# A DFT and two small MLPs on one core: the first weights' sums by DMA, their middle row by way of DRAM, another place for Qo's second operand and for the second MLP's PSUM tiles

## The chip, the cores and the metric

The kernel runs on one core of a Trainium2 chip. The metric is the time of one execution on the device, in microseconds. The engines are named as the profile names them: PE (TensorE, matrix products; PEld is its weight loading), DVE (VectorE), ACT (ScalarE), POOL (GpSimd), and SP, which mostly issues DMA transfers. POOL issues transfers too.

## The reference

The program takes `x` of 4 batches x 3072 positions x 256 channels and computes the real part of a two-dimensional DFT, then an MLP with a leaky activation, then a second MLP with a shift by one position and a gate.

```python
X = np.fft.fft(np.fft.fft(x, axis=1), axis=2).real
h = X @ w_in
X = np.maximum(0.01 * h, h) @ w_out
xk = mu_k * X + (1 - mu_k) * X_prev
xr = mu_r * X + (1 - mu_r) * X_prev
k = np.maximum(xk @ w_k, 0)
out = (k * k @ w_v) / (1 + np.exp(-(xr @ w_r)))
```

`X_prev` is X moved by one position, with zeros in front; the hidden widths are 2048 and 1024. The weights `w_in`, `w_out`, `w_k`, `w_v` and `w_r` arrive as float64, `x` as float32.

## The kernel before

**Products in two parts.** PE multiplies float32r operands. Where a product has to be exact to float32, each operand is split into a high and a low part (`hi_lo`: ACT copies the high part, DVE subtracts it, L90), and three products are added in PSUM: high by high, high by low, low by high.

**The DFT.** The transform along the 3072 positions is folded by symmetry into four real kinds, Pe, Qe, Po and Qo, each a set of matmuls with a table (`tab_a` to `tab_d`, 1158 KB each, loaded by POOL, L166). One kind is made in two halves, `fft_a` and `fft_b`, called at chosen units; `fft_src` splits the operands (t1Qo, sh1Qo, sl1Qo for batch 1), and DVE's L300 and L302 form the two classes of each kind (c1Po and the like). Pe has a middle row besides, which `fft_a` adds with one f32 matmul (L287, `e7p` by `altt`). The transform along the 256 channels isn't done by itself: it is multiplied into `w_in` at the start, by the tables `cet` and `sot` (matmuls L363 and L365 into `wps`), and the folded weights are kept as `woh`, `wol`, `weh`, `wel`.

**Units of the first MLP.** The four batches have four classes each (A1, A2, G1, G2), a class has 16 units of 128 hidden channels. `i` counts the 64 units of a batch. For each unit PE multiplies with Q (`mm_b`, 3 matmuls, L539), begins the next unit with P (`mm_a`, 3 matmuls, L527), and does the output product of an earlier unit (`outmm`, 12 matmuls, L550). Between these stand DVE's d (L591), ev (L532, for the next unit: a row of c times a column of `w128` is added, so it needs both) and gl (L571), and ACT's two leaky activations (L86) and gh (L83). PE's `mm_b` of a unit waits for that unit's ev.

**The boot.** There is no time in which the weights alone are loaded: the float64 weights are loaded in eight pieces each, converted and split while batch 0 is transformed and while the first class runs. `boot(u)` puts one step behind each of the first 16 units. A float64 piece goes through the steps `one` (ACT L108, DVE L110), `two` (DVE L116, makes fv), `three` (DVE L119, ACT L122, POOL L123, makes the small rest r), `four` (ACT L136 makes the high part, POOL L137 adds fv to r) and `five` (DVE L141 makes the low part). The column of `w128` for a piece of `w_in` is taken by `w_in_row`: PE multiplies the parts `wh` and `wl` with a column that is 1 in its first place only (L383, L384, four matmuls of two columns for a piece), and ACT copies the result.

**The second weights.** `w_k`, `w_v` and `w_r` make nine pieces, with the same five steps at one a unit: five pieces at units 53 to 57 of batches 0, 1 and 2 and at units 0 to 4 of batches 1 and 2, four in batch 3 from unit 8 on.

**The c rows.** Channel 128 of the folded channels has a row of its own: its transform along the positions is a row c, made by `c_a` and `c_b` (L405 to L417), stored to DRAM (L418) and spread over 128 partitions by `load_c`; its folded weights are the columns `w128`. ev adds the product of both.

**The second MLP** starts behind the last unit. `k_mm` (L854), `r_mm` (L904) and `v_mm` (L896) are its products. Its PSUM tiles are taken from a pool `ps2`, which is opened when the pools `ps_s` and `ps_o` of the first have been released, so its first `kps` waits for the last copies out of them (`flush`, yo). `do_prep(ti)` lists the steps that make the next tile's operands (mt, mx, mh, ml), and one step is taken a slot; a slot is the work around one `k_mm`, 12 matmuls.

All loops are unrolled. The order on each engine is that of the program; what an engine waits for is worked out from the tiles. The units at which the DFT's kinds stand, and the slots of the second MLP (f1 is that of `do_prep`), are these numbers:

```python
po_u, qo_u, f0, f1 = (2, 10, 17, 50) if b == 0 else (1, 4, 14, 50)
pe_u, qe_u = 53, 56
...
f0, f1, g0 = (0, 2, 4) if ti else (2, 5, 5)
```

Of the kernel before, what the change touches and what calls it, by code (L numbers as in the profile page):

```python
# [56 lines left out]
def fft_mlp_kernel(ctx, tc, xa, xb, x7, x8, x87, tb, tbs, alt, ce, so, mu, w_in, w_out, w_k, w_v, w_r, out):  # L57
# [5 lines left out]
    yd = [[[dram.tile([P, 2, JP], F32, name=f"y{b}_{c}_{s}") for s in range(2)] for c in range(4)] for b in range(B)]  # L63
    cd = dram.tile([B, 4, JP], F32, name="cd")

    ps_s = tc.alloc_tile_pool(name="ps_s", bufs=4, space=PSUM)
# [4 lines left out]
    w128 = misc.tile([P, NF], F32, name="w128")  # L71
    one0 = misc.tile([P, 2], F32R, name="one0")
    misc.tile([P, 112], F32, name="pad0")
    wp = tc.alloc_tile_pool(name="wp", bufs=1)
# [58 lines left out]
    def split_steps(z, k, f, parts):  # L133
        def four():
            z["p"] = parts()
            A.activation(z["p"][0], z["f"], ACTF.Copy, scale=2.0 ** -8)  # L136
            G.tensor_tensor(z["r"], z["r"], z["f"], op=ALU.add)  # L137

        def five():
            hi, lo = z["p"]  # L140
            V.scalar_tensor_tensor(lo, z["r"], 2.0 ** -8, hi.bitcast(F32), op0=ALU.mult, op1=ALU.subtract)  # L141
        return (*f64_steps(z, k, f), four, five)
# [114 lines left out]
    def fft_src(b, kind, h):  # L257
# [25 lines left out]
    def fft_a(b, kind):  # L283
        ps = ps_s.tile([P, 512], F32, tag="s", name=f"f{b}{kind}")
        fft_mm(b, kind, 0, ps, kind != "Pe")
        if kind == "Pe":
            T.matmul(ps[:, :JP], e7p, altt, start=False, stop=True)  # L287
        ev = work.tile([P, JP], F32, tag="fv", bufs=2, name=f"fe{b}{kind}")
        act_copy(ev[:, :JP], ps[:, :JP])
        return ps, ev  # L290
# [42 lines left out]
    uoh, uol = ([wp.tile([P, HF, D], F32R, name=n)] for n in ("uoh", "uol"))  # L333
    V.memset(one0.bitcast(F32), 0.0)
    V.memset(one0[0:1].bitcast(F32), 1.0)
    V.memset(altt, 0.0)
# [39 lines left out]
    def w_in_row(q):  # L376
        if q >= 8:
            return
        ps = win.pop(q)[0]
        for i in range(2):  # L380
            f = slice((2 * q + i) * P, (2 * q + i + 1) * P)
            o = ps[:, 2 * i:2 + 2 * i]
            T.matmul(o, woh[:, f], one0, start=True, stop=False)  # L383
            T.matmul(o, wol[:, f], one0, start=False, stop=True)  # L384
        act_copy(w128[:, 2 * q:2 * q + 2], ps[:, 0:4].rearrange("p (i t) -> p i t", t=2)[:, :, 0])

# [96 lines left out]
    ca = c_a(c8p, "a", True)  # L483
    w_in_row(1)
    w_in_parts(2)
    fft_b(0, "Pe", *pe)
    wout[0][1]()
    cs0 = c_b(c8p, "b", A1, *ca)
    cur_c = load_c(0, A1)
    wout[1][0]()  # L490
    qe = fft_a(0, "Qe")
    wout[0][2]()
    next_pair()
    w_in_parts(3)
    wout[1][1]()
    fft_b(0, "Qe", *qe)
    next_pair()
    cur = split_class(0, A1, "P") + split_class(0, A1, "Q")
    w_in_mm(2)


    def boot(u):
        q = u // 2
        if u % 2 == 0:
            w_in_row(q + 2)
            w_in_mm(q + 3)
            if 0 < q < 7:
                wout[q + 1][2]()
            if q < 6:
                wout[q + 2][0]()  # L510
            w_in_load(q + 4)
        else:
            w_in_split(q + 3)
            if q < 6:
                wout[q + 2][1]()
            w_in_parts(q + 4)
            w_out_load(q + 3)


# [238 lines left out]
    w_in_split(2)  # L758
    wout[1][2]()
    for b in range(B):  # L760

        po_u, qo_u, f0, f1 = (2, 10, 17, 50) if b == 0 else (1, 4, 14, 50)
        pe_u, qe_u = 53, 56
        done = 0
# [113 lines left out]
    wp.release()  # L878
    ps_o.release()
    ps_s.release()  # L880


    ps2 = ctx.enter_context(tc.tile_pool(name="ps2", bufs=1, space=PSUM))
    p2 = w2["p2"] = ctx.enter_context(tc.tile_pool(name="p2", bufs=2))
# [13 lines left out]
    def r_mm(xr, sig, m):  # L898
        hi, lo = xr
        ps = ps2.tile([P, 512], F32, tag="rps", bufs=2, name="rps")  # L900
        i = 0
# [21 lines left out]
    def drain():  # L923
        if q2:
            t, f, kk = q2.pop(0)
            if f == 0:
                t["v"] = [ps2.tile([P, 512], F32, tag="v", bufs=4, name=f"v{m}") for m in range(NB)]
            v_mm(f, kk, t["v"])
# [7 lines left out]
    for ti in range(len(tiles)):  # L936
        rd = ready.pop(ti)
        t = {"i": ti, "sig": p2.tile([P, NB, J], F32, tag="sig", name="sig")}
        end = ti == len(tiles) - 1
        f0, f1, g0 = (0, 2, 4) if ti else (2, 5, 5)  # L940
        if ti == 0:
            q1.append((t, 1, early[1][2]))
            q2.append((t, 0, kk0))
        for f in range(f0, NK):
            ps = ps2.tile([P, 512], F32, tag="k", bufs=2, name="kps")
            r = p2.tile([P, J], F32, tag="r", bufs=3, name="rl")
# [106 lines left out]
```

## Time and profile before

| | us |
|---|---|
| three runs | 1532.92, 1531.22, 1531.23 |
| median | 1531.23 |
| the profiled execution | 1529.78 |
| its span in the trace | 1528.0 |
| PE busy | 1499.0 (98%) |
| DVE busy | 1078.4 (71%) |
| ACT busy | 927.7 (61%) |
| POOL busy | 172.0 (11%) |

The span runs from the first to the last instruction of the trace; 1.78 us of the execution lie outside it. Busy times are sums over an engine's instructions, and a matmul is counted until its modelled end, so that two neighbours overlap: PE's idle time is best read from the list of its waits. A row of the timeline gives start, duration, engine, line, operation and operands, and in brackets the idle time of the engine ahead of it with what ended that. Names in rows leave buffer numbers out.

### The profile page before, as it was taken

Reading aid. Unit: us, or ns where it says so; the run is one execution under the profiler, and the core shown is the slowest. Engines: PE = TensorE matmul, PEld = TensorE weight load, DVE = VectorE, ACT = ScalarE, POOL = GpSimd, SP = SyncE. Lnnn points to the kernel's source line nnn. Section 1 sums busy time; section 2 is a strip of 40 time slices with the busy share of each in tenths; the row PEclk is TensorE's granted clock in tenths of the full one; section 3 lists DMA queues with packets and bytes.
Section 4 is the critical chain, followed back from the end, with each engine's and each line's share of the span. In section 5 each row is a group of like instructions: output and inputs, shape, how many; then the busy total and the mean of one; then the engine's idle time right before and its main releaser. Section 6 shows DMA issues by size and latency. Waiting matters only on the chain.

```text
span 1528.0 us, 22618 instructions
## 1 busy us (share of the span) xinstructions
PE 1499.0 (98%) x8490; PEld 1473.8 (96%) x8490; DVE 1078.4 (71%) x1798; ACT 927.7 (61%) x1785; POOL 172.0 (11%) x165
## 2 busy tenths in 40 slices
PE   5899999999999999999999999999999999999999
PEld 2789999999999999999999999999999999999998
DVE  7876767766667766667777666777677777776775
ACT  2666656656666665656566656666666666666664
POOL 4444201132101132001001000000000000000000
PEclk8999999999999999999999999999999999999999
DMA  7427405464214653124411002111111111111100
GB/s 249 156 83 149 82 10 164 129 153 90 55 27 152 183 119 56 40 75 138 137 54 47 21 1 73 42 42 42 42 42 42 42 42 42 42 42 42 42 22 32
DMA packets 74295, 116.34 MB, mean 76 GB/s; under 512 B 10798, under 2 KB 53822, under 8 KB 71114
## 3 DMA queue, kind: packets, MB, share of 16 engines
q1 hardware_dynamic: 51082, 74.62, 15.6%
q0 software_dynamic: 23104, 40.29, 11.8%
q8 instruction: 66, 1.08, 0.3%
q14 instruction: 43, 0.35, 0.1%
HBM read 87.06 MB, written 27.83 MB: 75 GB/s over the span
## 4 chain that ended last, share of the span: by engine, by line
PE 96%; DVE 2%; ACT 1%; issue 1%; DMA 0%; SPq 0%; POOL 0%; ACTq 0%; DVEq 0%
PE o L550 35%; PE kps L854 17%; PE v L896 17%; PE ps L539 9%; PE ps L527 9%; PE rps L904 4%; PE wps L363 0%; PE cps L405 0%; DMA xl<-in_xb 0%; PE cps L414 0%; PE f0Qo L280 0%; PE f0Po L280 0%; PE f1Qo L280 0%; PE f2Qo L280 0%; DVE fo L214 0%
## 5 line engine op out<-in xcount | busy, mean ns | idle before, releaser
L591 DVE SCALAR_TENSOR_TENSOR d<-ev,ps 128x384 f32<-128x384 f32 (+1 forms) x256 | 141.6, 553 | 195.8 <-PE ps L539 195.8
L83 ACT ACTIVATE gh<-g 128x768 fp32r<-128x768 f32 (+1 forms) x256 | 216.3, 845 | 69.7 <-PE o L550 67.7
L858 ACT ACTIVATE rl<-kps 128x384 f32<-128x384 f32 x254 | 124.9, 492 | 218.7 <-PE kps L854 218.7
L571 DVE TENSOR_TENSOR gl<-g,gh 128x768 fp32r<-128x768 f32 (+1 forms) x256 | 251.3, 982 | 1.3 <-ACT gh L83 1.0
L86 ACT ACTIVATE g<-ps 128x384 f32<-128x384 f32 (+1 forms) x256 | 125.9, 492 | 192.2 <-DVE d L591 191.2
L859 DVE SCALAR_TENSOR_TENSOR k<-kps,rl 128x384 f32<-128x384 f32 x254 | 141.5, 557 | 137.6 <-ACT rl L858 133.8
L550 PE MATMUL o<-gh,uoh 128*128 128x384 f32 (+1 forms) x1024 | 228.0, 337 | 0.0
L550 PE MATMUL o<-gl,uoh 128*128 128x384 f32 (+1 forms) x1024 | 227.7, 337 | 0.0
L550 PE MATMUL o<-gh,uol 128*128 128x384 f32 (+1 forms) x1024 | 227.6, 337 | 0.0
L550 PEld LDWEIGHTS o<-gl,uoh 128*128 128x128 f32 x1024 | 182.9, 188 | 0.0
L550 PEld LDWEIGHTS o<-gh,uoh 128*128 128x128 f32 x1024 | 182.6, 188 | 0.0
L550 PEld LDWEIGHTS o<-gh,uol 128*128 128x128 f32 x1024 | 182.5, 188 | 0.0
L532 DVE SCALAR_TENSOR_TENSOR ev<-cb,w,ps 128x384 f32<-128x384 f32 (+1 forms) x256 | 157.1, 614 | 0.0
L90 DVE TENSOR_TENSOR k2l<-k,k2h 128x384 fp32r<-128x384 f32 x254 | 139.6, 550 | 0.4 <-ACT k2h L83 0.4
L896 PE MATMUL v<-k2h,wvl 128*128 128x384 f32 x510 | 134.5, 334 | 0.0
L896 PE MATMUL v<-k2h,wvh 128*128 128x384 f32 x510 | 134.5, 334 | 0.0
L896 PE MATMUL v<-k2l,wvh 128*128 128x384 f32 x510 | 134.5, 334 | 0.0
L86 ACT ACTIVATE g<-d 128x384 f32<-128x384 f32 (+1 forms) x256 | 132.6, 518 | 0.0
L83 ACT ACTIVATE k2h<-k 128x384 fp32r<-128x384 f32 x254 | 131.7, 518 | 0.0
L854 PE MATMUL kps<-mh,wkh 128*128 128x384 f32 x508 | 129.1, 335 | 1.3 <-ACT mh L83 0.7
L854 PE MATMUL kps<-ml,wkh 128*128 128x384 f32 x508 | 129.0, 334 | 0.0
L854 PE MATMUL kps<-mh,wkl 128*128 128x384 f32 x508 | 128.9, 334 | 0.0
(377 smaller groups left out, 2551.0 us busy)
## 6 DMA issues: line engine op xcount, KB each, us to landing
out_dram<-o SPq DMA_DIRECT2D x31, 384.0 KB
y<-yo SPq DMA_DIRECT2D x24, 384.0 KB
tab_a<-in_tbs POOLq DMA_DIRECT2D x6, 1158.0 KB, 5.4
tab_b<-in_tbs POOLq DMA_DIRECT2D x6, 1158.0 KB, 5.9
tab_c<-in_tbs POOLq DMA_DIRECT2D x6, 1158.0 KB, 8.2
tab_d<-in_tbs POOLq DMA_DIRECT2D x6, 1158.0 KB, 5.7
xl<-in_xa SPq DMA_DIRECT2D x24, 256.0 KB
xa<-y SPq DMA_DIRECT2D x16, 384.0 KB
```

The lines of the kernel that those rows point to most:

```text
L83: A.activation(o, i, ACTF.Copy)
L86: A.activation(o, i, ACTF.Prelu, alpha=0.01)
L90: V.tensor_tensor(lo, src, hi.bitcast(F32), op=ALU.subtract)
L527: T.matmul(x["ps"][:, :n], l[:, f], r[:, :n], start=(i == 0), stop=(i == 2))
L532: V.scalar_tensor_tensor(x["ev"][:, :n], x["cb"][:, :n], w128[:, u:u + 1], x["ps"][:, :n], op0=ALU.mult, op1=ALU.add)
L539: T.matmul(x["ps"][:, :n], l[:, f], r[:, :n], start=False, stop=(i == 2), skip_group_check=True)
L550: T.matmul(po[s][h][:, :n], w[:, u % HF, h * P:(h + 1) * P], g[:, s, :n], start=(u == 0 and i == 0), stop=(u == NF - 1 and i == 2))
L571: V.tensor_tensor(gl[:, :, :n], x["g"][:, :, :n], x["gh"][:, :, :n].bitcast(F32), op=ALU.subtract)
L591: V.scalar_tensor_tensor(d[:, :n], x["ev"][:, :n], 2.0, x["ps"][:, :n], op0=ALU.mult, op1=ALU.subtract)
L854: T.matmul(ps[:, :J], w[:, k, sl], x[:, k], start=(i == 0), stop=(i == 5))
L859: V.scalar_tensor_tensor(k2, ps[:, :J], 0.0, r, op0=ALU.max, op1=ALU.mult)
L896: T.matmul(vps[m][:, :J], w[:, f, m * P:(m + 1) * P], x, start=(f == 0 and i == 0), stop=(f == NK - 1 and i == 2))
```

## The change

- `four` adds fv to r by a DMA that POOL issues (`accum_op=add`, 256 KB, from SBUF to SBUF) instead of a POOL instruction. This holds for the eight pieces of `w_out` and the nine of the second weights. In the boot, `five` moves from the even units to the odd ones, behind `w_in_split`.
- `w_in_row` has no matmuls: ACT copies row 0 of the PSUM tile, SP stores it to DRAM (`wd`), and `w_in_col`, a unit later, loads it back as a column.
- Fourteen matmuls on a tile of zeros ("warm") stand ahead of the first weights.
- The first c row is spread by a matmul with a row of ones (`spread_c`) and a copy by ACT, without DRAM.
- P of the first class is split behind `fft_b` of Pe instead of together with Q.
- Pe's middle row is multiplied in float32r for batches 1 to 3: two matmuls, for which ACT and DVE split `e7p`'s first row.
- Qo's unit goes from 4 to 5 (batches 1 to 3), Qe's from 56 to 57.
- The second MLP takes its PSUM tiles from the first's pools, and for tile 0 `do_prep(1)` comes at slot 4, not 5.

```diff
...
             A.activation(z["p"][0], z["f"], ACTF.Copy, scale=2.0 ** -8)
-            G.tensor_tensor(z["r"], z["r"], z["f"], op=ALU.add)
+            G.dma_start(z["r"], z["f"], accum_op=ALU.add)
...
         srcs[b, kind, h] = hi, lo
+        if kind == "Pe" and h == 0:
+            m = work.tile([1, 2, P], F32R, tag="fv", bufs=2, name=f"e7r{b}")
+            hi_lo(m[:, 0], m[:, 1], e7p[0:1])
+            a = work.tile([1, JP], F32R, tag="fv", bufs=2, name=f"altr{b}")
+            act_copy(a, altt[0:1])
+            srcs[b, "mid"] = m, a
...
         fft_mm(b, kind, 0, ps, kind != "Pe")
-        if kind == "Pe":
+        if kind == "Pe" and b == 0:
             T.matmul(ps[:, :JP], e7p, altt, start=False, stop=True)
+        elif kind == "Pe":
+            m, a = srcs.pop((b, "mid"))
+            for i in range(2):
+                T.matmul(ps[:, :JP], m[:, i], a, start=False, stop=(i == 1))
...
+
+    def spread_c(cs):
+        ps = ps_s.tile([P, 512], F32, tag="s", name="cbp")
+        T.matmul(ps[:, :JP], ones, cs[0:1, 0], start=True, stop=True)
+        t = pqp.tile([P, JP], F32, tag="cb", bufs=2, name="cb0_0")
+        act_copy(t[:, :JP], ps[:, :JP])
+        return t
+
...
             return
-        ps = win.pop(q)[0]
-        for i in range(2):
-            f = slice((2 * q + i) * P, (2 * q + i + 1) * P)
-            o = ps[:, 2 * i:2 + 2 * i]
-            T.matmul(o, woh[:, f], one0, start=True, stop=False)
-            T.matmul(o, wol[:, f], one0, start=False, stop=True)
-        act_copy(w128[:, 2 * q:2 * q + 2], ps[:, 0:4].rearrange("p (i t) -> p i t", t=2)[:, :, 0])
+        row = fft.tile([1, 256], F32, tag="x7", bufs=1, name="wr")
+        act_copy(row, win.pop(q)[0][0:1, 256:512])
+        Q.dma_start(wd[q:q + 1], row)
+
+    def w_in_col(q):
+        if q < 8:
+            Q.dma_start(w128[:, 2 * q:2 * q + 2], wd[q].rearrange("(i p) -> p i", p=P))
...
     vt, gt = (("g", 2), ("g", 2), ("yo", 2)), (("gh", 2), ("gl", 2), ("sd", 2))
+    zero = uoh[0][:, 0:2]
+    V.memset(zero.bitcast(F32), 0.0)
+    ones = work.tile([1, P], F32, tag="sd", bufs=2, name="ones")
+    G.memset(ones, 1.0)
...
     w_out_load(2)
+
+    ps = ps_s.tile([P, 512], F32, tag="s", name="warm")
+    for i in range(14):
+        T.matmul(ps, zero[:, 0, 0:P], zero, start=True, stop=True)
...
     pe = fft_a(0, "Pe")
     ca = c_a(c8p, "a", True)
     w_in_row(1)
+    w_in_col(0)
     w_in_parts(2)
     fft_b(0, "Pe", *pe)
+    cur = split_class(0, A1, "P")
     wout[0][1]()
+    w_in_col(1)
     cs0 = c_b(c8p, "b", A1, *ca)
-    cur_c = load_c(0, A1)
+    cur_c = spread_c(cs0)
     wout[1][0]()
     qe = fft_a(0, "Qe")
-    wout[0][2]()
     next_pair()
     w_in_parts(3)
     wout[1][1]()
+    wout[0][2]()
     fft_b(0, "Qe", *qe)
     next_pair()
-    cur = split_class(0, A1, "P") + split_class(0, A1, "Q")
+    cur += split_class(0, A1, "Q")
     w_in_mm(2)
     def boot(u):
         q = u // 2
         if u % 2 == 0:
+            w_in_load(q + 4)
             w_in_row(q + 2)
             w_in_mm(q + 3)
-            if 0 < q < 7:
-                wout[q + 1][2]()
             if q < 6:
                 wout[q + 2][0]()
-            w_in_load(q + 4)
         else:
             w_in_split(q + 3)
+            if q < 7:
+                wout[q + 1][2]()
             if q < 6:
                 wout[q + 2][1]()
             w_in_parts(q + 4)
             w_out_load(q + 3)
+            w_in_col(q + 2)
...
     w_in_split(2)
-    wout[1][2]()
...
-        po_u, qo_u, f0, f1 = (2, 10, 17, 50) if b == 0 else (1, 4, 14, 50)
-        pe_u, qe_u = 53, 56
+        po_u, qo_u, f0, f1 = (2, 10, 17, 50) if b == 0 else (1, 5, 14, 50)
+        pe_u, qe_u = 53, 57
...
     wp.release()
-    ps_o.release()
-    ps_s.release()
-
-
-    ps2 = ctx.enter_context(tc.tile_pool(name="ps2", bufs=1, space=PSUM))
+
+
...
             if f == 0:
-                t["v"] = [ps2.tile([P, 512], F32, tag="v", bufs=4, name=f"v{m}") for m in range(NB)]
+                t["v"] = [ps_o.tile([P, 512], F32, tag=f"o{t['i'] % 2}{m}", name=f"v{m}") for m in range(NB)]
...
         end = ti == len(tiles) - 1
-        f0, f1, g0 = (0, 2, 4) if ti else (2, 5, 5)
+        f0, f1, g0 = (0, 2, 4) if ti else (2, 4, 5)
...
         for f in range(f0, NK):
-            ps = ps2.tile([P, 512], F32, tag="k", bufs=2, name="kps")
+            ps = ps_s.tile([P, 512], F32, tag="s", name="kps")
...
```

The order of instructions moves at three places that matter. On DVE in the boot, from the classes of Pe to the first ev, this stood before (`c0Pe` and `c0Qe` are the classes, `cs` is the first c row, `Pl` and `Ql` the low parts of the first class, `uol` is what `five` writes):

```order
L417 SCALAR_TENSOR_TENSOR cs<-cev,cps 4x386
L110 TENSOR_SCALAR h<-h 128x512
L116 SCALAR_TENSOR_TENSOR fv<-st,h 128x512
L119 TENSOR_SCALAR h<-fv 128x512
L141 SCALAR_TENSOR_TENSOR uol<-r,uoh 128x512
L110 TENSOR_SCALAR h<-h 128x512
L116 SCALAR_TENSOR_TENSOR fv<-st,h 128x512
L119 TENSOR_SCALAR h<-fv 128x512
L302 SCALAR_TENSOR_TENSOR c0Qe_401<-fe0Qe,c0Qe_400 128x386
L90 TENSOR_TENSOR Pl_0_410<-c0Pe_352,Ph_0_409 128x386
L90 TENSOR_TENSOR Ql_0_414<-c0Qe_400,Qh_0_413 128x386
L532 SCALAR_TENSOR_TENSOR ev<-cb_0_365,w_105,ps 128x386
```

Here `five` (L141) stood between the two float64 pieces, and Pl next to Ql. On DVE at the same place there stands now:

```order
L90 TENSOR_TENSOR Pl_0_370<-c0Pe_365,Ph_0_369 128x386
L433 SCALAR_TENSOR_TENSOR cs<-cev,cps 4x386
L110 TENSOR_SCALAR h<-h 128x512
L116 SCALAR_TENSOR_TENSOR fv<-st,h 128x512
L119 TENSOR_SCALAR h<-fv 128x512
L110 TENSOR_SCALAR h<-h 128x512
L116 SCALAR_TENSOR_TENSOR fv<-st,h 128x512
L119 TENSOR_SCALAR h<-fv 128x512
L141 SCALAR_TENSOR_TENSOR uol<-r,uoh 128x512
L312 SCALAR_TENSOR_TENSOR c0Qe_421<-fe0Qe,c0Qe_420 128x386
L90 TENSOR_TENSOR Ql_0_430<-c0Qe_420,Qh_0_429 128x386
L560 SCALAR_TENSOR_TENSOR ev<-cb_0_385,w_106,ps 128x386
```

Pl has moved up ahead of cs, and `five` behind the steps of the next float64 piece. On POOL in batch 1's first units there stood (`tab_c` and `tab_d` are tables, `r` the rest of a float64 piece):

```order
L166 DMA tab_c_2922<-in_tbs 128x2316
L123 TENSOR_TENSOR r<-st,h 128x512
L166 DMA tab_d_3013<-in_tbs 128x2316
L137 TENSOR_TENSOR r<-r,fv 128x512
L166 DMA tab_a<-in_tbs 128x2316
```

The addition was POOL's own. On POOL at the same place there stands now:

```order
L166 DMA tab_c_2938<-in_tbs 128x2316
L123 TENSOR_TENSOR r<-st,h 128x512
L166 DMA tab_d_3029<-in_tbs 128x2316
L137 DMA r<-fv 128x512
L166 DMA tab_a<-in_tbs 128x2316
```

The addition has become a transfer, in the same queue as the tables. On DVE at this place there stood (`wl` is what `five` writes; `d`, `ev` and `gl` are a unit's):

```order
L300 SCALAR_TENSOR_TENSOR c1Po_3010<-fe1Po,c1Po_3009 128x386
L264 TENSOR_TENSOR t1Qo_3015<-pm_1042 128x384
L266 TENSOR_TENSOR t1Qo_3015<-x_1_1049 1x128
L90 TENSOR_TENSOR sl1Qo_3017<-t1Qo_3015,sh1Qo_3016 128x384
L591 SCALAR_TENSOR_TENSOR d<-ev,ps 128x386
L532 SCALAR_TENSOR_TENSOR ev<-cb_0_2360,w_105,ps 128x386
L571 TENSOR_TENSOR gl<-g,gh 128x2x386
L141 SCALAR_TENSOR_TENSOR wl<-r,wh 128x512
```

The operand t1Qo came right behind the class c1Po. On DVE at this place there stands now:

```order
L310 SCALAR_TENSOR_TENSOR c1Po_3026<-fe1Po,c1Po_3025 128x386
L619 SCALAR_TENSOR_TENSOR d<-ev,ps 128x386
L560 SCALAR_TENSOR_TENSOR ev<-cb_0_2370,w_106,ps 128x386
L599 TENSOR_TENSOR gl<-g,gh 128x2x386
L264 TENSOR_TENSOR t1Qo_3067<-pm_1052 128x384
L266 TENSOR_TENSOR t1Qo_3067<-x_1_1059 1x128
L90 TENSOR_TENSOR sl1Qo_3069<-t1Qo_3067,sh1Qo_3068 128x384
L141 SCALAR_TENSOR_TENSOR wl<-r,wh 128x512
L619 SCALAR_TENSOR_TENSOR d<-ev,ps 128x386
L560 SCALAR_TENSOR_TENSOR ev<-cb_0_2370,w_106,ps 128x386
```

The operand t1Qo has moved behind the d, ev and gl of a unit, with `five` behind it as before.

## Rows read from the trace of the kernel before

**Rows 1.** The page: busy time, share of the span and instructions of each engine.

```profile
PE 1499.0 (98%) x8490; PEld 1473.8 (96%) x8490; DVE 1078.4 (71%) x1798; ACT 927.7 (61%) x1785; POOL 172.0 (11%) x165
```

**Rows 2.** PE's waits in the whole run: line waited for, total us, times, longest.

```profile
PE wps L363 <- DVE fv L116: 14.7, 2, 8.2
...
PE f1Qo L280 <- ACT sh1Qo L83: 0.9, 1, 0.9
...
PE f2Qo L280 <- ACT sh2Qo L83: 0.9, 1, 0.9
```

**Rows 3.** Windows: span, then busy (count) of PE, PEld, DVE, ACT, POOL; clock; DMA.

```profile
62.00:110.00 48.00, 48.00 (x249) 41.17 (x248) 38.49 (x63) 30.67 (x60) 19.91 (x15) 1.00 0.30 95
```

**Rows 4.** Timeline of PE in the boot: start, duration, operation, count, [idle before <-releaser].

```profile
49.48 0.42 PE L539 MATMUL ps<-Qh,wh 128*128 128x386 f32 x1 [1.54 <-DVE ev L532]
...
50.62 0.17 PE L383 MATMUL wps<-one,wh 128*128 128x2 f32 x1
...
50.98 1.11 PE L363 MATMUL wps<-fv,cet 128*128 128x256 f32 x4
```

**Rows 5.** Timeline of the boot: ACT, POOL and DVE, same columns.

```profile
39.08 0.48 ACT L83 ACTIVATE cs<-cps 4x386 f32<-4x386 f32 x1 [1.03 <-PE cps L414]
...
46.80 1.59 POOL L137 TENSOR_TENSOR r<-r,fv 128x512 f32<-128x512 f32 x1
...
47.18 1.63 DVE L90 TENSOR_TENSOR Ql<-c0Qe,Qh 128x386 fp32r<-128x386 f32 x1
```

**Rows 6.** Timeline of all engines, batch 1's first units.

```profile
296.78 0.34 PE L539 MATMUL ps<-Qh,wh 128*128 128x386 f32 x1
...
297.25 0.58 POOL L166 DMA_DIRECT2D tab_d<-in_tbs  x1 [2.25 <-PE f1Po L280]
...
297.51 2.08 DVE L300 SCALAR_TENSOR_TENSOR c1Po<-fe1Po,c1Po 128x386 f32<-128x386 f32 x1 [1.69 <-ACT c1Po L83]
...
297.85 1.31 POOL L137 TENSOR_TENSOR r<-r,fv 128x512 f32<-128x512 f32 x1
...
302.98 0.34 PE L539 MATMUL ps<-Qh,wh 128*128 128x386 f32 x1
...
303.35 0.68 DVE L141 SCALAR_TENSOR_TENSOR wl<-r,wh 128x512 fp32r<-128x512 f32 x1
...
306.16 0.33 PE L539 MATMUL ps<-Qh,wh 128*128 128x386 f32 x1
```

**Rows 7.** Landing of Pool's transfers: a page row, then min/median/max of line L202.

```profile
tab_d<-in_tbs POOLq DMA_DIRECT2D x6, 1158.0 KB, 5.7
...
L202 POOL DMA_DIRECT2D xl<-in_xb x18: 1073/1091/1859, 119.5 to 611.3; - x18
...
DMA to landing us min/median/max: 4.3/4.9/9.5
```

**Rows 8.** Line L166 from 320.9 to 321.5 with its landing; timeline of POOL behind it.

```profile
L166 POOL DMA_DIRECT2D tab_b<-in_tbs x1: 947/947/947, 321.0 to 321.0; - x1
...
DMA to landing us min/median/max: 8.9/8.9/8.9
...
322.39 1.80 POOL L202 DMA_DIRECT2D xl<-in_xb  x1
```

**Rows 9.** Timeline of POOL and DVE, a weight piece in batch 3.

```profile
760.92 1.49 POOL L137 TENSOR_TENSOR r<-r,fv 128x512 f32<-128x512 f32 x1
...
766.57 0.56 DVE L591 SCALAR_TENSOR_TENSOR d<-ev,ps 128x386 f32<-128x386 f32 x1 [0.56 <-PE ps L539]
```

**Rows 10.** Timeline of PE around Pe's middle row, batch 0's last units.

```profile
244.32 0.81 PE L287 MATMUL f1Pe<-altt,e7p 128*128 128x386 f32 x2
...
245.14 0.34 PE L539 MATMUL ps<-Ql,wh 128*128 128x384 f32 x1
```

**Rows 11.** Timeline of PE at the second MLP's start.

```profile
925.36 0.62 PE L854 MATMUL kps<-mh,wkh 128*128 128x384 f32 x2 [0.58 <-ACT yo L83]
...
941.25 0.61 PE L854 MATMUL kps<-mh,wkh 128*128 128x384 f32 x2 [0.74 <-ACT mh L83]
```

More of the change, by code (lines that the diff above doesn't have):

```diff
@@ L64, in fft_mlp_kernel @@
     cd = dram.tile([B, 4, JP], F32, name="cd")
+    wd = dram.tile([8, 256], F32, name="wd")
     ps_s = tc.alloc_tile_pool(name="ps_s", bufs=4, space=PSUM)
@@ L71, in fft_mlp_kernel @@
     w128 = misc.tile([P, NF], F32, name="w128")
-    one0 = misc.tile([P, 2], F32R, name="one0")
-    misc.tile([P, 112], F32, name="pad0")
+    misc.tile([P, 120], F32, name="pad0")
     wp = tc.alloc_tile_pool(name="wp", bufs=1)
@@ L333, in fft_mlp_kernel @@
     uoh, uol = ([wp.tile([P, HF, D], F32R, name=n)] for n in ("uoh", "uol"))
-    V.memset(one0.bitcast(F32), 0.0)
-    V.memset(one0[0:1].bitcast(F32), 1.0)
     V.memset(altt, 0.0)
@@ L899, in r_mm @@
         hi, lo = xr
-        ps = ps2.tile([P, 512], F32, tag="rps", bufs=2, name="rps")
+        ps = ps_s.tile([P, 512], F32, tag="s", name="rps")
         i = 0
@@ L976, in fft_mlp_kernel @@
         w2[k].release()
+    ps_o.release()
+    ps_s.release()
 def dft_tables():
```

## The prediction

> **What bounds the kernel now.** I read the page first. TensorE (PE) is busy 98% of the span, 1499.0 us [rows 1], VectorE (DVE) 71% and ScalarE (ACT) 61%; so a change is worth what it takes from PE's own work or from PE's idle time, and work of other engines counts only where PE comes to wait for it. The list of PE's waits says where the idle time lies: 14.7 us of it in two waits for the first folded-weight matmuls, before any table has come, and 0.9 us in each of batches 1 and 2 on the second operand of Qo [rows 2]. The windows then separate the stages: between 62 and 110 us PE has no gap at all (48.00 of 48.00), with 0.30 of the DMA in use [rows 3]. There an instruction taken from PE shortens the run by its own length, and a wait put in lengthens it. Before 62 us PE and the three vector engines pass work to and fro [rows 4, 5], and a gain must survive every hand-over. The last views are the timelines of two places with gaps, batch 1's first units [rows 6] and the second MLP's start [rows 11].
>
> All sums are made against the profiled run, 1529.78 us; the median of the three runs is 1531.23, and I carry the difference over unchanged. A difference under 0.2%, 3.1 us, is one that a measurement of this kernel can't tell from none.
>
> **The change part by part.**
>
> *Boot, up to 62 us.* The f32 matmul that spreads the first c row stands between the matmuls of cps and those of f0Qe, and it waits for ACT's cs. Before, f0Qe followed cps at once, at about the time at which cs started, 39.0; cs ends at 39.56 [rows 5]. One group of four row matmuls falls out ahead of it, 50.98 − 50.62 = 0.36 [rows 4], so cs ends at about 39.2 now. The spreading matmul has no row of its own; its nearest is Pe's middle row, also f32 with 386 columns: 0.65 us (below, [rows 10]). f0Qe then starts at 39.85: +0.9 at this point, and Qh and Ql behind it are later by as much, less the 0.5 that Ph no longer takes on ACT ahead of Qh. Ql started at 47.18 and took 1.63 us while POOL's sum ran beside it [rows 5]; d, with as many elements, takes 0.56 [rows 9]. With the sum off POOL, Ql runs from 47.6 to 48.1, ev to 48.7, and unit 0's mm_b, which had to wait 1.54 us for that ev [rows 4], starts then instead of at 49.48: 0.8 ahead. Two more row groups (0.36 each) are gone before 62: 1.5 ahead at best. DVE and POOL don't get ahead by as much, so PE's later waits on them grow; I keep **−0.9**, and from −1.9 (every small wait gone) to +0.6 (the spreading matmul's 0.9 stays and only one row group is felt).
>
> *Four row groups behind 62 us.* Four of the eight stand where PE is full [rows 3, 4]: 4 × 0.36 = **−1.4**. The row now goes ACT, DRAM, column; ACT and SP have the time (ACT's share is in [rows 1]), and a column is asked for two units before its use.
>
> *Pe's middle row in float32r.* From 244.32 to the second matmul behind it is 0.82, of which one matmul of 0.18 is that behind it: 0.65 for the f32 row. A unit's 18 float32r matmuls take 306.16 − 302.98 = 3.18 [rows 6], 0.177 each; two are 0.35. Three batches × 0.29 = **−0.9**. The three small ACT copies and one DVE operation for it lie in a unit that has room: nothing.
>
> *Qo a unit later.* A unit's start at 296.78 comes back at 302.98, 6.20 later. One unit (3.18) and the nine matmuls of f1Qo (9 × 0.177 = 1.59) explain 4.77: 1.43 are lost, first to c1Po on DVE, 2.08 us long because POOL's sum began at 297.85 beside it, then to the operand behind c1Po [rows 6]. With a unit more of room, and no sum on POOL, this goes; batch 2 has the same wait [rows 2]. 2 × 1.43 = **−2.9**.
>
> *The sums by DMA.* POOL's seventeen additions become transfers that add 256 KB in SBUF. Most are asked for a unit or more before DVE's subtraction (`five`) needs them, in the boot over ten us before for most pieces: nothing. Two are close, in batch 1 and 2 at unit 3. POOL issues tab_d at 297.25, the sum behind it at 297.85 [rows 6]; `five` now waits for a transfer, and behind it on DVE stand d and ev of the next unit, for which PE waits. PE reaches that ev's use at 296.78 + 2 × 3.18 + 1.59 = 304.73. DVE needs about 1.7 from `five` to the end of that ev (0.68 for `five` [rows 6], 0.56 for d [rows 9] and as much again for ev, a little overlapped). So the sum must have landed by 303.0, 5.2 us after its issue. The trace shows no sum inside SBUF. Its nearest row is Pool's sum from DRAM of the same 256 KB, L202: 4.3 to 9.5 us to landing, median 4.9 [rows 7]. But here a table of 1158 KB, 5.7 us to landing [rows 7], stands ahead of it, landing at 302.95. One such pair is in the trace: tab_b at 321.00, 8.9 to landing, and a sum issued behind it at 322.39 [rows 8], which is the 9.5 of L202; it landed 2.0 after the table, behind another of 128 KB. 256 KB alone at tab_d's rate are 5.7 × 256/1158 = 1.3 us, so our sum lands at 304.2: 1.2 late, twice: **+2.4**. The ends: nothing (4.9 after issue is in time), and 2 × (9.5 − 5.2) = +8.6.
>
> L202's issue on POOL took 1.07 us in the middle and 1.86 at most [rows 7], 0.8 more. The Trainium skill, DMA: Bandwidth & Descriptors, section SWDGE vs HWDGE vs iDMA, says that GpSimd writes such descriptors into SBUF and that VectorE's two-port mode shuts it out of there; that speaks against the change. No row ties the 1.86 to it; by that rule I would add at most 0.8 to each of the two sums, 1.6 in all, which stands inside the ends above.
>
> *Second MLP's start.* Without the release of the pools, kps doesn't wait for the copy yo, idle 0.58; and the second operand, mh, comes a slot sooner (12 matmuls, 2.1 us), which is more than PE's wait for it, 0.74 idle [rows 11]. A matmul is listed with 0.34 where the next starts 0.177 behind it [rows 6], so each such gap really takes 0.16 more: 0.58 + 0.74 + 0.32 = 1.6. The pairs at these waits take 0.62 and 0.61 instead of 0.34 + 0.177 = 0.52, and mh's second half comes behind its first; for that I add 0.4. Together **−2.0**, from −1.0 (mh is held up elsewhere) to −2.2.
>
> *At nothing:* the fourteen dummy matmuls, which fill part of the 14.7 us in which PE waits for weights [rows 2]; if that cover is gone they cost what reaches past the first weights, under 2 us. Qe a unit later: its successors are not waited for.
>
> Sum: −0.9 − 1.4 − 0.9 − 2.9 + 2.4 − 2.0 = **−5.7**: a profiled run of 1524.1, a median of **1525.5**.
>
> **The rivals.**
>
> *A: the two sums land in time.* For it: L202's median of 4.9 is under 5.2 [rows 7], and a transfer within SBUF has no DRAM to wait for. Against it: the table ahead in the same queue. The 2.4 goes: −8.1, **1523.1**. The Trainium skill, same page, section Queues, rings and completion order, says that each DMA engine takes descriptors in ring order; by that rule A falls, and the one pair in the trace agrees, its sum 2.0 us behind its table [rows 8].
>
> *B: the two sums are as late as L202's slowest.* 9.5 us instead of 6.4: −5.7 − 2.4 + 8.6 = +0.5, **1531.7**, no difference. For it: the 9.5 was seen behind a table [rows 8]; against it: that table itself took 8.9, tab_d here 5.7.
>
> *C, slower: sums within SBUF are slow in themselves.* Then not two, but all nine w2 pieces hold up DVE. In batch 3 the sum was issued at 760.92, d started at 766.57 [rows 9]; PE's next use is about 2.6 later, less DVE's 1.7: the sum is needed by 767.5, 6.6 after issue. With seven such pieces and the two at 5.2, a landing of x us costs 2(x − 5.2) + 7(x − 6.6) against the gain of 8.1: even at x = 7.2, slower by over 0.2% from 7.5 on, and at 9.5 it is 8.6 + 20.3 − 8.1 = +20.8, **1552**. Against it: no row here is that slow in the middle.
>
> *D: the boot change does nothing or loses, all else as forecast.* The spreading matmul's 0.9 is not given back: 1.5 us later, 1527.0; that lies inside the forecast.
>
> **How the numbers follow.** The forecast (with D) 0.52, A 0.22, B 0.16, C 0.10. The forecast's own range, with the boot from −1.9 to +0.6 and the second MLP from −1.0 to −2.2, is 1524.3 to 1528.0. The range of 8 in 10 goes down through A with a good boot, 1521.9, and up to half of B's way, 1530.0; it leaves out C and the later half of B. Faster by over 0.2% (below 1528.2): the forecast and nearly all of A, 0.73; within 0.2%: most of B, 0.16; slower: C and a little of B, 0.11.
>
> **What would show it.** In the changed profile: PE's waits on sh1Qo, sh2Qo, yo and mh are gone, and no small matmuls with 2 columns are left. c1Po takes 0.56. In batch 1 and 2 a wait of PE for ev of about 1.2 stands near 304 and at the like place of batch 2, with DVE's `five` ended late by a DMA: that decides between the forecast, A and B. If DVE waits for DMA at `five` in batch 3 as well, C is right. The boot is right if f0Po starts near 61.2. I would be wrong if TensorE's granted clock fell in a stretch where it was full before, since PE's rows would then lengthen all over that stretch.

## The result, and where it went

The changed kernel takes 1541.82 us, the median of four runs (1541.13 to 1543.13), against 1531.22: a ratio of 1.0071, with an interval of 1.0059 to 1.0083, 10.6 us slower. I had forecast 1525.5 and a range that ended at 1530.0. The profiled execution has a span of 1539.7 us, 11.7 more than before.

PE's busy time grows by 5.9 us, and the chain shows the new thing: besides PE, which falls from 96% to 92%, DMA stands in it with 3%. From the page after, as [rows 1] before, and the chain's line:

```profile
PE 1504.9 (98%) x8474; PEld 1479.2 (96%) x8474; DVE 1073.8 (70%) x1800; ACT 930.8 (60%) x1792; POOL 160.4 (10%) x166
...
PE 92%; DVE 3%; DMA 3%; issue 1%; POOL 1%; ACT 0%; SPq 0%; POOLq 0%; ACTq 0%; DVEq 0%
```

The list of PE's waits after answers [rows 2] (line waited for, total us, times, longest):

```profile
PE ps L567 <- DVE ev L560: 13.7, 7, 3.5
PE wps L379 <- DVE fv L116: 10.1, 2, 8.7
PE f0Pe L293 <- DVE e7p L238: 3.0, 1, 3.0
```

The waits for sh1Qo, sh2Qo, yo and mh are gone, as forecast. In their place PE waits 13.7 us in seven places for ev, up to 3.5 us at a time. Before, the waits for ev were 2.3 us in two places.

Where PE stands at the start of each unit's second operand (its first L539 or L567 matmul), after less before, splits the difference by place:

| from | to | us |
|---|---|---|
| start | unit 0 | −1.8 |
| unit 0 | unit 3 | +1.7 |
| unit 3 | unit 11, the row groups | −1.3 |
| units 53 to 60 of batches 0 to 2 (the middle row) | | +0.2 |
| units 62 and 63 of batches 0 to 2 | | +5.2 |
| units 4 to 8 of batches 1 and 2: Qo's wait gone | | −2.9 |
| the same units: sums | | +12.5 |
| the rest of the first MLP | | 0.0 |
| the second MLP | | −2.0 |

The total is +11.7 (the entries are rounded). Two entries carry it. The first is batch 1's unit 6; the timeline after, as [rows 6] before:

```profile
297.62 0.57 POOL L166 DMA_DIRECT2D tab_d<-in_tbs  x1 [2.26 <-PE f1Po L286]
...
297.88 0.56 DVE L310 SCALAR_TENSOR_TENSOR c1Po<-fe1Po,c1Po 128x386 f32<-128x386 f32 x1 [1.70 <-ACT c1Po L83]
...
298.61 0.90 POOL L137 DMA_DIRECT2D r<-fv  x1 [0.41 <-issue]
...
307.04 0.69 DVE L141 SCALAR_TENSOR_TENSOR wl<-r,wh 128x512 fp32r<-128x512 f32 x1 [4.81 <-DMA r<-fv]
...
308.78 0.69 PE L567 MATMUL ps<-Qh,wh 128*128 128x386 f32 x1 [3.54 <-DVE ev L560]
...
314.74 0.36 PE L567 MATMUL ps<-Qh,wh 128*128 128x386 f32 x1
```

c1Po takes 0.56 instead of 2.08, and t1Qo stands a unit later: the gain that was forecast. But DVE's `five` (wl) sits 4.81 us for the sum, with d and ev behind it, and PE waits 3.54. The chain from 298.61 to 308.78 is this sum, then `five`, d and ev.

The sum took 8.41 us from its issue at 298.61 to the landing; I had worked out 6.35 from an issue at 297.85. The table ahead of it had landed 7.2 after its own issue, not 5.7. Line L137's answer for all seventeen sums (duration on POOL, who waited, landing min/median/max), and the answer for that one table:

```profile
L137 POOL DMA_DIRECT2D r<-fv x17: 862/891/1012, 38.4 to 850.0; - x17
...
  DVE wl L141: 10.3, 4
...
  DVE gl L599: 2.7, 2
...
DMA to landing us min/median/max: 3.3/4.1/8.8
```

```profile
L166 POOL DMA_DIRECT2D tab_d<-in_tbs x1: 574/574/574, 297.6 to 297.6; - x1
...
DMA to landing us min/median/max: 7.2/7.2/7.2
```

Then comes a loss that I had not counted. The windows after (span; busy time and count of PE, PEld, DVE, ACT, POOL; granted clock; DMA share; GB/s) begin with the wait:

```profile
304.00:308.70 4.70, 1.25 (x8) 0.93 (x6) 1.66 (x4) 0.47 (x2) 0.56 (x1) 0.92 0.80 204
308.80:310.80 2.00, 2.00 (x6) 2.00 (x7) 1.35 (x2) 1.52 (x4) 0.00 (x0) 0.50 0.96 334
310.80:314.60 3.80, 3.80 (x13) 3.80 (x13) 2.52 (x4) 2.22 (x4) 0.00 (x0) 0.50 0.51 195
314.70:318.00 3.30, 3.30 (x20) 3.30 (x20) 2.02 (x3) 0.91 (x2) 1.75 (x2) 0.99 0.80 231
```

Behind 4.7 us in which PE was busy 1.25, the granted clock is 0.50, that is 1.2 GHz, until 314.6, and PE goes through one whole unit at that level: 314.74 − 308.78 = 5.96 where a unit takes 3.18 [rows 6], 2.8 us in each of the two batches (in batch 2 the wait is 3.02 and the unit behind it takes 5.95).

The second entry is unit 62. The row that comes from DRAM for c1Qe is asked for 1.8 us later than before, because Qe stands a unit later, and lands at about 272.7. The first two rows are before, the others after:

```profile
266.66 0.54 SPq L308 DMA_DIRECT2D c1Qe<-cd  x2
...
271.46 0.53 ACT L83 ACTIVATE Qh<-c1Qe 128x386 fp32r<-128x386 f32 x1 [0.79 <-DMA c1Qe<-cd]
```

```profile
268.48 0.53 SPq L318 DMA_DIRECT2D c1Qe<-cd  x2
...
272.78 0.53 ACT L83 ACTIVATE Qh<-c1Qe 128x386 fp32r<-128x386 f32 x1 [2.93 <-DMA c1Qe<-cd]
...
273.34 0.56 DVE L90 TENSOR_TENSOR Ql<-c1Qe,Qh 128x386 fp32r<-128x386 f32 x1 [3.03 <-ACT Qh L83]
...
274.94 0.44 PE L567 MATMUL ps<-Qh,wh 128*128 128x384 f32 x1 [1.38 <-DVE ev L560]
```

Qh on ACT and Ql on DVE wait for it, in places that did not move; DVE's d and ev stand behind Ql, and PE waits 1.38, 1.41 and 1.58 in the three batches.

### The profile page after: what moved, and what is told of

It is laid out like the page before. It is cut to its first block, busy times and chain, and to the rows that moved or that the text cites. A ratio compares the mean times of both kernels' runs of the same rounds, so it can differ in the third digit from the quotient of the medians.

```text
span 1539.7 us, 22644 instructions
## 1 busy us (share of the span) xinstructions
PE 1504.9 (98%) x8474; PEld 1479.2 (96%) x8474; DVE 1073.8 (70%) x1800; ACT 930.8 (60%) x1792; POOL 160.4 (10%) x166
## 4 chain that ended last, share of the span: by engine, by line
PE 92%; DVE 3%; DMA 3%; issue 1%; POOL 1%; ACT 0%; SPq 0%; POOLq 0%; ACTq 0%; DVEq 0%
PE o L578 33%; PE v L920 17%; PE kps L881 17%; PE ps L567 8%; PE ps L555 8%; PE rps L928 4%; DMA r<-fv 2%; POOL r L123 0%; DMA xl<-in_xb 0%; DMA c3Qe<-cd 0%; DVE fe L213 0%; DMA c2Qe<-cd 0%; DMA c1Qe<-cd 0%; DVE d L619 0%; PE cps L430 0%
## 5 line engine op out<-in xcount | busy, mean ns | idle before, releaser
L599 DVE TENSOR_TENSOR gl<-g,gh 128x768 fp32r<-128x768 f32 (+1 forms) x256 | 247.5, 967 | 4.1 <-DMA r<-fv 2.7
```

The source lines that it names most:

```text
L599: V.tensor_tensor(gl[:, :, :n], x["g"][:, :, :n], x["gh"][:, :, :n].bitcast(F32), op=ALU.subtract)
```

## The experiments

All times are medians; the kernel before took 1530.71 to 1530.82 in their runs. First the sums.

**Second weights' sums on POOL again.** Only `four` of these nine pieces changes:

```diff
-            G.dma_start(z["r"], z["f"], accum_op=ALU.add)
+            if z.get("w2"):
+                G.tensor_tensor(z["r"], z["r"], z["f"], op=ALU.add)
+            else:
+                G.dma_start(z["r"], z["f"], accum_op=ALU.add)
```

> The changed kernel with the nine sums of the second weights as POOL instructions again; the sums of the first weights stay transfers. Theory: the two sums behind a table (8.3 and 8.4 us to landing) cost 3.6 us of wait each at unit 6 of batches 1 and 2, and behind each wait PE runs a unit at the lower clock, some 2.8 us more; both go: 1541.8 - 12.8 = 1529.0, and PE's clock is 1.00 around 310. Rival 1 (only the wait goes, the clock falls for another reason): 1534.6. Rival 2 (POOL's instruction beside DVE gives back c1Po's 2.08 us and with it the wait for Qo): 1531 to 1532.

Measured: 1532.53 us, ratio to before 1.0016 (1.0006 to 1.0025): 9.3 below the changed kernel. In the trace the step at units 5 to 8 falls by 5.7 and 5.2, and the low clock is gone with the wait (1.00 from 304 to 315). It is short of the 12.8 because POOL's addition again takes part of Qo's gain, 0.7 in each batch (below), and in this profile because PE is 1.0 later at unit 3. The first rival, 1534.6, falls; the second named the remainder rightly, and the time lies 0.5 above the range that it gave.

**The sum ahead of the table.** The same transfer, in another place of POOL's queue:

```diff
+                if b > 0 and i == 3:
+                    w2_steps.pop(0)()
                 for kb, kind, k_u in ((b, "Po", po_u), (b, "Qo", qo_u), (b + 1, "Pe", pe_u), (b + 1, "Qe", qe_u)):
...
-                    if pe_u <= i < pe_u + 5 or (b > 0 and i < 5):
+                    if pe_u <= i < pe_u + 5 or (b > 0 and i < 5 and i != 3):
```

> The changed kernel, in which only the step that issues the sum at unit 3 of batches 1 and 2 stands ahead of that unit's part of the DFT, so that the transfer is queued on POOL ahead of table d and about 3 us sooner. Theory (the table ahead in the queue makes it late): it lands 3.3 to 5 us after issue, near 300, DVE's low part doesn't wait, PE doesn't either: 1541.8 - 12.8 = 1529.0. Rival (a sum of 256 KB at this place is slow by itself, from other loads): 8.4 us to landing again, at about 304, a wait of about 1 us and no fall of the clock: near 1531 to 1533, with the landing time on the row telling it.

Measured: 1531.95 us, ratio 1.0006 (0.9997 to 1.0016), 9.9 below. Its timeline, and the landing of the sum at 300.36:

```profile
300.36 0.93 POOL L137 DMA_DIRECT2D r<-fv  x1 [0.77 <-POOL r L123]
...
301.84 0.56 POOL L166 DMA_DIRECT2D tab_d<-in_tbs  x1 [0.55 <-PE f1Po L286]
...
DMA to landing us min/median/max: 4.3/4.3/4.3
```

A sum of the same size, asked for 1.5 us ahead of the table and not 1.0 behind it, lands in 4.3 us. In the trace units 5 to 8 gain 6.5 and 5.9 us against the changed kernel, 12.4 in all, as expected. Two other places of this profile take some of it back: PE is 2.3 later at unit 3, and 1.9 more go at units 62 and 63 of batch 0. There PE waits 1.76 for ev (1.38 in the changed kernel), and the unit behind takes 282.39 − 277.62 = 4.77 instead of 3.25, with the granted clock at 0.65 (last row: a window):

```profile
277.62 0.45 PE L567 MATMUL ps<-Qh,wh 128*128 128x384 f32 x1 [1.76 <-DVE ev L560]
...
282.39 0.36 PE L567 MATMUL ps<-Qh,wh 128*128 128x384 f32 x1
...
277.60:282.40 4.80, 4.78 (x19) 4.78 (x20) 2.84 (x4) 2.98 (x5) 0.00 (x0) 0.65 0.00 0
```

So the place in the queue made the sums late, and not their kind.

**Qe's unit back at 56.**

```diff
-        pe_u, qe_u = 53, 57
+        pe_u, qe_u = 53, 56
```

> The changed kernel with Qe's unit back at 56, all else as changed. Theory: Qe a unit later makes the c1Qe row land one unit too late for Qh and Ql, which stand on DVE ahead of d and ev of unit 62; in the changed trace the wait is 1.38 us of PE at 274.94, and unit 62 falls back by 1.5 to 1.7 us in each of three batches. So 1541.8 - 4.7 = 1537.1. Rival (that wait only takes up slack that comes back elsewhere, as the sums' waits follow it): no change, 1541.8.

Measured: 1554.18 us, ratio 1.015 (1.0135 to 1.0165), 12.4 *above* the changed kernel. Both theory and rival fall. The timeline at unit 59 of batch 0:

```profile
256.16 0.58 POOL L166 DMA_DIRECT2D tab_c<-in_tbs  x1 [0.41 <-PE f1Qe L286]
...
256.73 0.92 POOL L137 DMA_DIRECT2D r<-fv  x1
...
265.45 0.69 DVE L141 SCALAR_TENSOR_TENSOR wl<-r,wh 128x512 fp32r<-128x512 f32 x1 [5.21 <-DMA r<-fv]
...
267.66 0.69 PE L567 MATMUL ps<-Qh,wh 128*128 128x384 f32 x1 [3.98 <-DVE ev L560]
```

With Qe at 56 the sum of that unit stands behind table c, lands after 8.7 us, and PE waits 3.98, 3.96 and 3.86 in the three batches, each time with a stretch at the lower clock behind it: against the kernel before, units 59 and 60 together take 6.9, 5.8 and 6.5 more. The wait at unit 62 does go (−1.5). So Qe's later unit was part of the sums' price: it kept a third place free of tables and paid 5.2 us for that.

**Both undone together, once with POOL, once with the order.** Kernel `e5_pool_qe56` has the POOL additions, Qe at 56 and the f32 middle row. Kernel `e6_first_qe56` has transfers everywhere, Qe at 56, and the step that issues the sum ahead of the table at both units:

```diff
-        pe_u, qe_u = 53, 57
+        pe_u, qe_u = 53, 56
...
+                if len(w2_steps) > 5 * (len(sources) - n_early) and (i == 56 or (b > 0 and i == 3)):
+                    w2_steps.pop(0)()
...
-                    if pe_u <= i < pe_u + 5 or (b > 0 and i < 5):
+                    if (pe_u <= i < pe_u + 5 and i != 56) or (b > 0 and i < 5 and i != 3):
```

> The changed kernel with the nine second-weight sums as POOL instructions, Qe's unit at 56 and Pe's middle row in f32 again. The run with Qe at 56 alone came out at 1554.2 because there the sum at unit 56 stood behind table c (8.7 us to landing); with no transfers for these sums, Qe at 56 costs nothing and the wait at unit 62 is gone. Theory: 1532.5 (the run with POOL's sums) less three waits of 1.55 and less 0.2 for the middle row: 1527.7, faster than before by 0.2%. Rival (POOL's sums put the waits of before back, and the wait at unit 62 only moves): 1531 to 1532.

> The changed kernel with all sums as transfers and Qe's unit at 56, in which the step that issues the sum stands ahead of that unit's part of the DFT both at unit 3 and at unit 56, so that no sum is queued behind a table. Theory (only the place in the queue made the sums late): every sum of the second weights lands within 5 us, no wait for ev is left at units 59, 62 and 6, and the time is 1532.0 (sum first at unit 3) less 4.7: 1527.3. Rival (sums are late there whatever the order, from other loads): 1537 or more, with the landing of the sum near 257 over 6 us.

Measured: 1526.50 (0.9975, 0.9965 to 0.9985) and 1525.92 (0.9965, 0.9952 to 0.9979). Both are faster than the kernel before; the second, the changed kernel less two faults of order, is 4.8 below the kernel before; I had forecast 5.7 for the change. PE's largest waits in its list are the boot's alone, and in the two windows that answer to the waits after, where the changed kernel's clock was granted to 0.77 and 0.83, PE is full at 1.00:

```profile
PE wps L379 <- DVE fv L116: 9.8, 2, 8.9
PE f0Pe L293 <- DVE e7p L238: 3.7, 1, 3.7
PE ps L567 <- DVE ev L560: 2.7, 2, 2.0
```

```profile
300.00:315.00 15.00, 15.00 (x87) 15.00 (x86) 10.23 (x19) 7.73 (x15) 0.53 (x1) 1.00 0.78 260
520.00:540.00 20.00, 20.00 (x115) 20.00 (x115) 13.88 (x22) 12.03 (x23) 7.76 (x8) 1.00 0.77 194
```

**Useless matmuls in the wait.** To see whether the idle time is what lowers the clock, PE gets work that nobody needs, and the wait stays:

```diff
+                if b in (1, 2) and i == 6:
+                    wps_ = ps_s.tile([P, 512], F32, tag="s", name="fill")
+                    for _ in range(16):
+                        T.matmul(wps_[:, 0:384], x["w"][0][:, 0:P], x["w"][0][:, 0:384], start=True, stop=True)
                 step(x, nx)
```

> The changed kernel with sixteen matmuls more, of no use, ahead of unit 6's second operand in batches 1 and 2, at the place where PE waits 3.5 us for ev; they read operands that have long been there and take about 2.8 us. Theory (the idle time, and not something else, makes the clock fall behind it): the unit behind runs at 1.00, 2.8 us come back in each batch: 1541.8 - 5.6 = 1536.2, though PE does more. Rival (the clock falls for another reason, or the matmuls reach past the wait): 1541.8 or more.

Measured: 1537.59 us, 1.005 (1.0036 to 1.0064), 4.2 below the changed kernel, although PE does more. The timeline and the window behind the wait:

```profile
306.52 2.94 PE L809 MATMUL fill<-Ph 128*128 128x384 f32 x16
...
310.04 0.44 PE L567 MATMUL ps<-Qh,wh 128*128 128x386 f32 x1 [0.57 <-DVE ev L560]
...
313.32 0.34 PE L567 MATMUL ps<-Qh,wh 128*128 128x386 f32 x1
```

```profile
308.80:314.60 5.80, 5.23 (x30) 4.91 (x29) 5.19 (x10) 4.09 (x8) 0.00 (x0) 1.00 0.88 325
```

The wait ends where it did, but the unit behind it takes 313.32 − 310.04 = 3.28 instead of 5.96 and the clock is 1.00. In the trace the step at unit 7 falls by 2.7 in both batches. The difference to the expected 5.6 is the boot of that profile, 1.3 us slower at unit 3. So the idle time costs twice: 3.5 us itself and 2.8 behind it.

**The steps that were to gain, alone.** The second MLP's part on the kernel before (the PSUM hunks and slot 4 of the diff above):

> The kernel before with the second MLP's part of the change alone: PSUM tiles from the first MLP's pools, the next operand's steps a slot sooner. Theory: the waits for yo and mh go, 0.58 and 0.74 in the list with the gaps around them: 2.0 less than before, 1528.7. Rival (the wait for mh moves to another operand or to the sigmoid's table load): 0.8 less, 1530.

Measured: 1528.99, ratio 0.9990 (0.9981 to 0.9998): 1.7 less. PE is full where it was not; windows from 917 to 960, before and with this part:

```profile
917.00:960.00 43.00, 41.65 (x235) 40.46 (x234) 26.83 (x48) 28.03 (x57) 0.00 (x0) 1.00 0.23 65
```

```profile
917.00:960.00 43.00, 43.00 (x248) 42.76 (x247) 27.83 (x49) 28.88 (x58) 0.00 (x0) 1.00 0.21 65
```

Qo's unit alone, on the kernel before (5 for 4 in the tuple):

> The kernel before with Qo's unit alone moved from 4 to 5 (batches 1 to 3). The prediction's step: the wait for Qo's operand goes in two batches, 2 x 1.43 = 2.9 less, 1527.8. Theory now (POOL's addition still runs beside c1Po, as in the run with POOL's sums, where each batch gained 0.64 and not 1.34): 1.3 less, 1529.4. Rival (nothing is gained while POOL adds): 1530.7.

Measured: 1529.50, ratio 0.9992 (0.9983 to 1.0001): 1.3 less. The wait for Qo's operand is gone, but c1Po, with 2.08 us, is as slow as before, and d and ev now stand right behind it, so that PE waits for ev at unit 5 instead:

```profile
300.82 0.45 PE L539 MATMUL ps<-Qh,wh 128*128 128x386 f32 x1 [0.51 <-DVE ev L532]
```

In the trace each batch gains 0.65 and not 1.43. The other half belongs to POOL's addition beside DVE: with the transfer in its place (`e6_first_qe56`) each batch gains 1.42. The transfer with Qo still at 4 wasn't run.

The middle row in f32 again, on `e6_first_qe56` (both `if` lines of that hunk taken back):

> The kernel with all sums ahead of the tables and Qe at 56 (1525.9), with Pe's middle row in one f32 matmul again. The prediction's step (float32r saves 0.29 in three batches): 0.9 more, 1526.8. Theory from the traces (the step of units around 54 shows +0.28 and then -0.21, so the two float32r matmuls cost 0.07 more than the one in f32): 0.2 less, 1525.7, which the times can't tell from none; the trace's rows decide.

Measured: 1526.38, no difference that the times can tell. In its trace the step around unit 54 is −0.28 and then +0.21 of `e6_first_qe56`, in each of three batches: 0.07 less. The prediction's step was wrong.

**The boot.** Three kernels, of which none moved the time beyond its spread: the first weights' sums on POOL again in the changed kernel, the same on `e6_first_qe56` (both by `if not z.get("w2")` in the first diff), and that kernel without the dummy matmuls (`range(0)` for `range(14)`).

> The changed kernel with the eight sums of the first weights as POOL instructions again; those of the second weights stay transfers. Theory: in the boot gl of the first two units waits on DVE for a sum (1.86 and 0.80 us, landing 8.8 us after issue), which makes the weights' matmuls at 58.7 wait; without it the boot keeps the 1.8 us that it is ahead at unit 0: 1541.8 - 1.7 = 1540.1. Rival (POOL's additions slow DVE down by the same amount): 1541.8.

> The kernel with all sums ahead of the tables and Qe at 56 (1525.9), with the eight sums of the first weights as POOL instructions again. Theory (in the boot a sum that lands 8.8 us after its issue holds gl up, but POOL's addition slows DVE down by about as much): no difference, 1525.9. Rival (the late sums in the boot cost 1.7 us net): 1524.2.

> The kernel with all sums ahead of the tables and Qe at 56 (1525.9), without the fourteen dummy matmuls at the start. Theory (the dummies are done long before the stretch whose clock differs from run to run, from 24 to 36 us; c_a took 2.11 in three profiles and 3.46 to 3.72 in three others with them): no difference, 1525.9, within a spread of 2 us that the boot has anyway. Rival (they keep the clock up in the boot): c_a's six matmuls take 3.5 or more in every run, 1.4 to 1.7 more, 1527.5.

Measured: 1542.48 (the changed kernel: 1541.82); 1526.28; 1526.12 (`e6_first_qe56`: 1525.92). The 1.7 us that the first was to give back are not seen. Single profiles differ more than these medians: c_a's matmuls take from 2.11 us, at the full clock, to 3.80, partly at the lower level, with the dummies and without them (2.11 in five profiles of fourteen, two of them without). The first of these rows is without them, the second with them:

```profile
29.61 2.11 PE L421 MATMUL cps<-tab_a,c8p 128*4 128x386 f32 x6
```

```profile
29.66 3.72 PE L421 MATMUL cps<-tab_a,c8p 128*4 128x386 f32 x6
```

## Why the prediction was wrong, step by step

*The sums.* The step that failed is the 2.4 us for two late sums; they cost 12.5. The place, the waiting line and the deadline were right: the sum landed at 307.02 and PE waited 3.54, so it was needed at 303.5, and I had said 303.0, with the whole kernel standing 0.4 later there by now. Two numbers of the landing were wrong. The first is the table ahead, which took 7.2 to landing and not 5.7 (7.0 in batch 2, where it had taken 5.5 before). I had taken a table with little beside it. In the changed kernel a store of 256 KB from SP (w_1h, 298.39) is issued 0.8 behind the table and the sum 1.0 behind it, and the DMA engines are busy 0.98 between 300 and 304. In `e8_qo5` and `e2_w2pool`, where the store comes 0.8 behind too but POOL adds, the table takes 6.3 and 6.5; in the kernel before, the store comes only 4.3 behind. So about half of the 1.5 us goes with the store, which Qo's later unit had brought forward, and the rest with the sum. The second number is the sum's own part: it landed 2.2 behind the table (1.9 in batch 2), not 1.3, nearly the 2.0 of the pair in [rows 8], which I had set aside for a bandwidth estimate; that row had stood for exactly this case.

Rival B, with 9.5 us, was nearer, and its 4.3 us each are not far from the waits of 3.5 and 3.0 seen. But B's sum, like mine, left out the 2.8 us that PE loses at 1.2 GHz behind each wait. The profile before had shown the clock at its lower level only in the boot, behind idle PE: there a wait of 3.1 us for e7p ends at 29.11, the granted clock is 0.53 from 30.0 to 33.6, and c_a's six matmuls take 3.80 instead of 2.11. I had kept the clock for a sentence at the end.

Rival A, that the sums land in time, falls: the same sum lands 4.3 us after its issue ahead of the table and 8.4 behind it. The Trainium skill, DMA: Bandwidth & Descriptors, section Queues, rings and completion order, says that each DMA engine takes descriptors in ring order; these two landings agree with it, though the page says it of the queues of SP and ACT, and these are POOL's transfers. Rival C falls too: the sums of batch 3 land in 3.3 to 3.4 us and hold nobody up. The same page of the Trainium skill, section SWDGE vs HWDGE vs iDMA, says that VectorE's two-port mode shuts GpSimd out of its descriptors; no such delay is seen here, where a sum's issue on POOL took 0.86 to 1.01 us in all seventeen cases.

*Qe a unit later*, at nothing, cost 5.2. The step that failed is "its successors are not waited for": I had followed the matmuls of Qe, and not the transfer that its class starts and that Qh and Ql wait for at a unit that stays where it is. In the trace before, ACT had waited 0.79 us for that transfer, so there was no room for a unit's delay.

*The middle row*, −0.9, was +0.2. I priced the float32r pair by the pace of matmuls in a full row of them:

```profile
242.77 0.33 PE L286 MATMUL f1Pe<-tab_a,sl1Pe 128*128 128x386 f32 x1
243.03 0.61 PE L297 MATMUL f1Pe<-altr,e7r 1*128 1x386 f32 x2
243.57 0.44 PE L567 MATMUL ps<-Qh,wh 128*128 128x384 f32 x1
243.85 0.34 PE L567 MATMUL ps<-Ql,wh 128*128 128x384 f32 x1
```

The pair's turn comes at 242.95, one pace of 0.177 behind the matmul ahead of it, and Ql's matmul starts at 243.85; less one pace for Qh's, the pair took 0.73 and not 0.35. It starts 0.08 late and is followed late; that it has one row of weights instead of 128 may be why, but no run shows it. The one f32 matmul took 0.65 [rows 10].

*Qo*, −2.9, was right in the changed kernel, and both causes that I had named make it: the unit alone gives 1.3 by the times, and the rest comes when the sum leaves POOL as well. *The row groups*, −1.4, gave −1.3. *The second MLP*, −2.0, gave −2.0 in the changed kernel and 1.7 alone. *The dummies*, at nothing: no difference is seen without them, in a spread of 5 us.

*The boot*, −0.9, gave −0.1 in this pair of profiles, and here the reading is weak. f0Po, which I had put near 61.2, starts at 62.04 (62.12 before). PE was 1.8 ahead at unit 0, nearly all of it c_a at the higher clock, which other profiles lack; then DVE's gl waited for a sum that landed 8.8 us after its issue:

```profile
30.08 2.11 PE L421 MATMUL cps<-tab_a,c8p 128*4 128x386 f32 x6
...
47.71 0.42 PE L567 MATMUL ps<-Qh,wh 128*128 128x386 f32 x1 [1.54 <-DVE ev L560]
...
55.34 0.96 DVE L599 TENSOR_TENSOR gl<-g,gh 128x772 fp32r<-128x772 f32 x1 [1.86 <-DMA r<-fv]
...
58.71 1.10 PE L379 MATMUL wps<-fv,cet 128*128 128x256 f32 x4 [1.38 <-DVE fv L116]
```

Between unit 0 and unit 3 PE fell back by 1.7 us. I had looked at who waits for a sum in `five`, and not at gl, whose buffer the sum reads. How much of the 1.7 is the late sum's isn't shown: in `e4_bootpool` and `e12_bootpool`, where gl waits for no transfer but POOL adds beside DVE, PE still falls back by 1.3 there against the kernel before. It also stays open what sets the clock level in the boot from run to run, and with it whether the boot's part of the change gains anything; no run has that part alone. At unit 3, PE stands between 0.7 ahead of the profile before and 3.7 behind it in the eleven profiles with the changed boot, and 0.2 and 2.3 behind it in the two others with the old boot: they show no gain.

## What to carry to other kernels

A transfer that takes the place of an instruction has a place in a queue, and what stands ahead there is part of its duration: list for each one what its queue and the other queues move at that moment, and issue it ahead of bulk loads that nobody waits for soon. Where a change may make PE wait in a stretch that was full, look at what the granted clock does behind such waits elsewhere in the trace, and price that too; here it was 2.8 us on top of 3.5. And when a step is moved, follow its transfers to the instructions that wait for them, since those may not move along.

## What the runs showed that I had not expected

A sum of 256 KB from SBUF to SBUF landed 3.3 us after its issue where nothing else moved (batch 3), 3.3 to 5.4 beside other transfers, 5.7 to 8.8 in the boot's first three, and 7.9 to 8.7 behind a table of 1158 KB. PE's clock went to 1.2 GHz behind a wait of some 3.5 us in otherwise full work and stayed there for 5.8 us of full work; with sixteen useless matmuls in that wait it stayed at 2.4 GHz. A wait of 1.76 us in another run was followed by lower clock too (0.65 over 4.8 us), while behind one of 1.38 in the changed kernel it stayed at 1.00. Two float32r matmuls with one row of weights took 0.73 us, more than one f32 matmul with 128 rows.
